# Attention and squared-ReLU MLP in one kernel: the last x rows copied on chip, plain x operands not stored, second weight group later, products in groups of 2, 3, 2

## The chip, the cores and the metric

One core of one Trainium2 chip. The metric is the device time of one execution in microseconds (us), as the median of several runs. TensorE (PE) multiplies, VectorE (DVE) and ScalarE (ACT) work elementwise, GpSimd (POOL) does elementwise work too, and SyncE (SP) issues the DMA transfers.

## The reference

```python
def _attn_ref(q, k, v, w1, b1, w2):        # q, k, v: 4 x 8 x 576 x 64
    scores = scale * np.matmul(q, k.transpose(0, 1, 3, 2))
    ...
    scores = scores + bias.transpose(2, 0, 1)[None, :, :, :]
    scores = scores - np.max(scores, axis=-1, keepdims=True)
    attn = np.exp(scores)
    attn = attn / (np.sum(attn, axis=-1, keepdims=True) + 1e-09)
    return np.matmul(attn, v)

def _moe_ref(x, w_in, w_out, s, b):        # x: 2304 x 512, w_in: 512 x 2048, w_out: 2048 x 512
    h = x @ w_in
    r = np.maximum(h, 0.0)
    g = s * (r * r) + b
    return g @ w_out
```

The attention's result, heads side by side, is the x of the second part.

## The kernel before

**Attention.** Heads and batches are worked off in 16 pairs of two batches of one head; `step(n)` issues a fifth of a pair for each of the engines. The last four pairs are (batches 0 and 1: head 6, head 7) and (batches 2 and 3: head 6, head 7). `norm_store` and `norm_load` (L327, L335) send the reciprocal row sums through memory (`rs`) and spread them over the partitions (`rb`). `av` (L409) multiplies by v in five groups of matmuls into `xps` (L422, L425); after the last group DVE multiplies by `rb` (L428, L429), and `store_xt` (L403) stores the result, transposed, as rows of `xt_d`.

**Second part.** The 2304 tokens are three pairs of chunks p = 0, 1, 2 of 768 tokens, the 2048 hidden units four groups g of 512. `items` lists the 12 steps (g, p): (0,0), (0,1), (1,1), (1,0) and so on. An item has two halves s, and a half is seven products in the order 1, 6, 5, 7, 2, 3, 4 (`ORDER`): a Strassen scheme in which x and w_in stand as seven operands each, four of them sums (T1 to T4 of x, S1 to S4 of w_in), three of them plain blocks (products 1, 2 and 3). Each operand is split into a high and a low part (ACT copies the high part, `x_hi` L587, `w_hi` L532; DVE subtracts, `x_lo` L591, `w_lo` L536), and a product (`product`, L604) is six matmuls of 384 columns at L614. `quad_posts` (L619) combines the four banks of a half: `keep` copies bank a before product 2 adds to it (ACT, L636), `u2` (DVE, L640), `v` reads bank b before product 3 adds to it (DVE, L645), `c22` reads bank d before product 4 adds to it (DVE, L648), and relu, square, affine and the split into `gt` follow. `project` (L711) multiplies `gt` by w_out: a block is three matmuls of 512 columns (L720), twelve blocks in each half of the following item. `evict` (L731) takes a finished `o` out of PSUM: ACT copies it in a chunk pair's first item (L738), DVE adds afterwards (L740).

**Operands and weights.** `load_x` (L559) loads a pair's x from `xt_d` into `x_in(p)`: into the weights' raw buffer `big` for p = 0, into `wd` otherwise. All seven split operands of p = 0 and 1 are stored to `xs_d` (`store_x`, 768 KB each) and come back by `reload_x` where a later item needs them. A weight group is loaded raw (`load_w`, L467), decoded in four passes (`decode_w`: ACT L476, POOL L478, DVE L480, L483, L486), and split; w_out's low part is POOL's (`wout_lo`, L507). Two buffers take turns for the decoded w_out, so the decoding of its third block waits for the low part of the first.

**The order.** It is written out by hand. The loop at L1087 counts slots T, seven to a half; a slot issues its product, its share of the twelve blocks (`SHARE`, L1086), and what `at(slot, ...)` has booked for it (`fire`). Item n starts at slot 14 n. A booking sets an instruction's place in its engine's queue; each engine works its queue in order and waits at an instruction whose inputs are not there. The first products of item 0 are issued between the last steps of the attention (L955 to L982).

Of the kernel before, what the change touches and what calls it, by code (L numbers as in the profile page):

```python
# [26 lines left out]
def attention_moe(ctx, tc, q, k, v, w_in, w_out, dist, par, out):  # L27
# [375 lines left out]
    def store_xt(p):  # L403
        h, b0 = pairs[p]
        xs = xts.pop(p)
        for x in range(2):
            nc.sync.dma_start(out=xt_d[b0 // 2][x, h * D:(h + 1) * D, :], in_=xs[64 * x:64 * x + 64, :])

# [150 lines left out]
    def load_x(p, a):  # L559
        t0, done = 2 * CH * p, 0  # L560
        while done < 2 * CH:
            b, o = divmod(t0 + done, S)
            w = min(2 * CH - done, S - o)
            nc.sync.dma_start(
                out=x_in(p)[:, a, done:done + w],
                in_=xt_d[b // 2][b % 2, 128 * a:128 * a + 128, o:o + w])
            done += w
# [387 lines left out]
    next(att)  # L955
    next(att)
# [32 lines left out]
    mix["wd"] = op.tile([128, 3, 1024], U32, name="wd")  # L989
# [12 lines left out]
    for n in range(1, NI + 1):  # L1002
        for j in range(2):
            for t, o in enumerate((4, 5, 7)):
                at(14 * n + 7 * j + o, lambda n=n, j=j, t=t: evict(n - 1, 1 - j, t), 0)

    def fresh_x(n, q, free):
        base = 14 * n
        for a in range(KB):
            at(base, lambda a=a: load_x(q, a))  # L1010
        for o, name in ((5, "T1"), (6, "T2"), (8, "T3"), (11, "T4")):
            for e in range(2):
                at(base + o, lambda name=name, e=e: x_sum(q, name, e, nc.vector, free))
        for i, m in enumerate(ORDER):
            o = base + (7 + i if i > 0 else 6)
            at(o, lambda m=m: x_new(q, m))
            for e in range(2):
                at(o, lambda m=m, e=e: x_hi(q, m, e))
            for e in range(2):
                at(o + 1, lambda m=m, e=e: x_lo(q, m, e, free))  # L1020
            if q < 2:
                at(o + 2, lambda m=m: store_x(q, m))

    def fresh_w(g):
        base = 28 * (g - 1)
        start = [base + (9 if g == 1 else 7), base + 20]
# [5 lines left out]
        for kind in range(2):  # L1032
            for i in range(4):
                k, t0 = 4 * kind + i, start[kind] + 3 * i
# [5 lines left out]
                if g == 1 and kind == 0:  # L1040
                    at(base + 4 + i // 2, lambda e=(kind, g, i): load_w(*e))
                elif g == 1 and i == 0:
                    at(base + 17, swap_raw, 1)
                    for x in range(3):
                        at(base + 17, lambda e=(kind, g, x): load_w(*e))
                elif g == 1 and i < 3:
                    pass
                else:
                    at(t0 - 7 if k < 3 else t0 - 6, lambda e=(kind, g, i): load_w(*e))
                at(t0 - 2, begin)  # L1050
                at(t0 - 1, lambda k=k: next(decs[k]))
                for x in range(3):
                    at(t0 + x, lambda k=k: next(decs[k]))
                if kind == 1:
                    at(t0 + 3, lambda i=i: wout_hi(g, i, nc.scalar))
                    at(t0 + 3, lambda i=i: wout_lo(g, i))
                    if g < 3:
                        at(t0 + 5, lambda i=i: store_wo(g, i))
        for name, o in (("S1", 21), ("S2", 21), ("S3", 24), ("S4", 26)):
            at(base + o, lambda name=name: w_sum(name, nc.vector), 1)  # L1060
        for i, m in enumerate(ORDER):
            at(base + 22 + i, lambda m=m: w_hi(m, nc.scalar))
            at(base + 23 + i, lambda m=m: w_lo(m, nc.vector))
            if g < 3:
                at(base + 25 + i, lambda m=m: store_wi(g, m))

    for i, m in enumerate(ORDER):
        at(i + 2, lambda m=m: store_x(0, m), 1)
# [3 lines left out]
    for n in range(1, NI - 1):  # L1072
# [4 lines left out]
        elif p1 != p:  # L1077
            for i, m in enumerate(ORDER):
                at(base + (7 + i if i > 0 else 2), lambda p1=p1, m=m: reload_x(p1, m))
# [6 lines left out]
    SHARE = (2, 2, 2, 2, 2, 1, 1)  # L1086
# [73 lines left out]
```

## Time and profile before

| | us |
|---|---|
| median of 3 runs | 671.68 (671.26 to 672.03) |
| the profiled execution | 668.71 |
| its span, first to last instruction | 666.8 |
| PE busy with matmuls | 635.6 (95%) |
| DVE busy | 500.7 (75%) |
| ACT busy | 437.5 (66%) |
| POOL busy | 184.0 (28%) |
| mean granted clock of PE | 0.985 |

The profile's page gives each engine's busy time, the span in 40 slices of 16.7 us, the chain of work that ended last, and the costliest groups of instructions by line. The timeline lists instructions in order of time; in brackets stands how long the engine was idle before one, and what ended that. An engine's next row starts where the one before it leaves the pipeline, so what an instruction costs in a busy stretch is the distance of two starts.

### The profile page before, as it was taken

To read this page: it belongs to the slowest core of one execution; us is meant where nothing else is said; L and a number is where in the kernel's file an instruction comes from. 1 tells how busy PE (TensorE), PEld (TensorE's weight loads), DVE (VectorE), ACT (ScalarE), POOL (GpSimd) and SP (SyncE) were. 2 spreads that over 40 slices of the span, in tenths; PEclk is the share of its full clock that TensorE was granted. 3 is DMA by queue.
4 is the path that set the end of the run, shared out by engine and by line. 5 is a ranking of instruction groups with operands and counts; after the bars stand their busy time and mean duration, and the time that the engine had idled before them with its cause. 6 is when DMAs were issued, how large, how long until landed. Compare 5 with 4: busy or idle time off the path is not lost.

```text
span 666.8 us, 14496 instructions
## 1 busy us (share of the span) xinstructions
PE 635.6 (95%) x5418; PEld 510.9 (77%) x5418; DVE 500.7 (75%) x1063; ACT 437.5 (66%) x927; POOL 184.0 (28%) x208
## 2 busy tenths in 40 slices
PE   8999989999999999759899999999999999999997
PEld 5667566666666665548788988889888898988886
DVE  7988888999999987666996798779648654445552
ACT  7988777888887787464886666457447544554440
POOL 7992332535668624011240122112100000000000
PEclk9999998999999999959999999999999999999999
DMA  6978688576877874699389269811361156546302
GB/s 183 329 236 280 211 268 279 170 259 208 278 262 248 268 246 149 202 402 389 142 321 385 85 251 328 314 57 61 140 240 48 64 197 229 180 167 204 144 0 95
DMA packets 54034, 142.00 MB, mean 213 GB/s; under 512 B 10445, under 2 KB 13517, under 8 KB 53965
## 3 DMA queue, kind: packets, MB, share of 16 engines
q1 hardware_dynamic: 53628, 140.82, 60.8%
q8 instruction: 43, 0.70, 0.4%
q10 hardware_dynamic: 208, 0.26, 0.1%
q14 instruction: 27, 0.21, 0.1%
q0 software_dynamic: 128, 0.00, 0.0%
HBM read 92.04 MB, written 49.02 MB: 212 GB/s over the span
## 4 chain that ended last, share of the span: by engine, by line
PE 70%; DMA 10%; DVE 8%; ACT 5%; issue 3%; POOL 3%; SPq 1%; DVEq 0%; ACTq 0%; POOLq 0%
PE o L720 28%; PE hps L614 23%; PE bps L170 5%; PE xps L422 5%; PE sps L277 5%; DMA qt<-in_q_dram 4%; PE tps L350 3%; ACT pr L310 3%; DMA big<-in_moe_w_in_dram 2%; DVE tt L299 1%; DMA wd<-in_moe_w_out_dram 1%; ACT pt L378 1%; DMA rs<-rt 1%; POOL kr L250 1%; DMA kt<-in_k_dram 1%
## 5 line engine op out<-in xcount | busy, mean ns | idle before, releaser
L720 PE MATMUL o<-wo,gt 128*128 128x512 f32 x864 | 224.9, 394 | 0.0
L614 PE MATMUL hps<-x,wi 128*128 128x384 f32 x1008 | 207.3, 342 | 14.0 <-ACT h L636 5.7
L614 PEld LDWEIGHTS hps<-x,wi 128*128 128x128 f32 x1008 | 182.7, 191 | 33.4 <-ACT h L636 6.2
L720 PEld LDWEIGHTS o<-wo,gt 128*128 128x128 f32 x864 | 159.7, 188 | 24.0 <-DVE gt L695 0.3
L310 ACT ACTIVATE pr<-tt,mn 128x576 f32<-128x576 f32 x144 | 110.7, 770 | 38.8 <-DVE mn L299 38.5
L299 DVE CUSTOM_DVE_ANT_0 tt<-sps,bt 128x576 f32<-128x576 f32 x128 | 91.4, 750 | 10.0 <-PE sps L277 8.7
L350 PEld LDWEIGHTS tps<-ident,pr 64*128 64x128 f32 x1216 | 44.5, 138 | 45.0 <-issue 20.1
L422 PE MATMUL xps<-pt,vt 128*64 128x256 f32 (+1 forms) x512 | 76.8, 421 | 1.0 <-PE xps L422 1.0
L277 PE MATMUL sps<-kr,qr 64*128 64x288 f32 x768 | 73.3, 309 | 3.1 <-POOL kr L250 2.7
L659 ACT ACTIVATE h<-hps 128x384 f32<-128x384 f32 x24 | 11.7, 488 | 83.8 <-PE hps L614 83.8
L277 PEld LDWEIGHTS sps<-kr,qr 64*128 64x128 f32 x768 | 58.9, 188 | 4.6 <-POOL kr L250 3.4
L350 PE MATMUL tps<-ident,pr 64*128 64x64 f32 x1216 | 56.1, 230 | 5.8 <-ACT pt L378 4.1
L678 ACT ACTIVATE h<-h,sb 128x384 f32<-128x384 f32 x72 | 50.8, 706 | 10.7 <-DVE h L674 9.3
L380 DVE COPY pt<-tps 128x512 f32<-128x512 f32 x64 | 43.8, 684 | 9.2 <-PE tps L350 8.7
L740 DVE TENSOR_TENSOR acc<-o,acc 128x512 f32<-128x512 f32 x36 | 24.8, 689 | 31.0 <-PE o L720 29.9
L422 PEld LDWEIGHTS xps<-pt,vt 128*64 128x64 f32 x512 | 31.2, 136 | 21.2 <-issue 9.5
L695 DVE TENSOR_TENSOR gt<-h,gt 128x384 fp32r<-128x384 f32 x72 | 41.6, 578 | 6.6 <-ACT gt L686 6.6
L170 PE MATMUL bps<-f,pt__127 128*32 128x79 f32 (+44 forms) x640 | 39.7, 390 | 2.2 <-POOL f L139 1.4
L686 ACT ACTIVATE gt<-h 128x384 fp32r<-128x384 f32 x72 | 37.8, 525 | 2.3
L137 DVE TENSOR_SCALAR f<-lg,thr 128x432 f32<-128x432 f32 (+9 forms) x68 | 39.2, 653 | 0.0
L170 PEld LDWEIGHTS bps<-f,pt__127 128*32 128x32 f32 x640 | 24.0, 109 | 17.9 <-issue 6.4
L378 ACT ACTIVATE pt<-tps 128x512 f32<-128x512 f32 x64 | 36.9, 577 | 0.0
(137 smaller groups left out, 798.8 us busy)
## 6 DMA issues: line engine op xcount, KB each, us to landing
x<-xs SPq DMA_DIRECT2D x21, 768.0 KB
wid<-wi SPq DMA_DIRECT2D x21, 512.0 KB
xs<-x SPq DMA_DIRECT2D x14, 768.0 KB
wi<-wid SPq DMA_DIRECT2D x21, 512.0 KB
bias<-stg SPq DMA_DIRECT2D x36, 295.5 KB
bt<-bias SPq DMA_DIRECT2D x7, 1152.0 KB
kt<-in_k_dram SPq DMA_DIRECT2D x16, 464.0 KB
wod<-wo SPq DMA_DIRECT2D x12, 512.0 KB
```

The costliest lines, as they stand in the source:

```text
L170: nc.tensor.matmul(pb[32 * c:32 * c + 32, base + a:base + b], w2bd, mov, start=True, stop=True)
L277: nc.tensor.matmul(o, a, b, start=(i == 0), stop=(i == 2))
L299: nc.vector.tensor_tensor_reduce(tt.rearrange("p (a b) -> p a b", a=2), ps[x][:, :, 0:HALF], bias.rearrange("p (a b) -> p a b", a=2), -1.0 ...
L310: nc.scalar.activation(pr[:, x], tts.pop((n, x)), AF.Exp, bias=mn[:, x:x + 1], scale=-1.0, accum_out=sums[p][:, col // 3, col % 3:col % 3 ...
L350: nc.tensor.matmul(outs[r], src[d], ident[d, d], is_transpose=True, start=start, stop=True, skip_group_check=not start)
L378: nc.scalar.activation(o, i, AF.Copy)
L380: nc.vector.tensor_copy(o, i)
L422: nc.tensor.matmul(o, vt[:, 4 * x + kb, :], pt[:, kb, x, c], start=(i == 0), stop=(i == 4))
L614: nc.tensor.matmul(ps, w_ops[m][:, w, k, s], xo[p, m][:, x, k], start=(first and i == 0), stop=(i == 5), skip_group_check=not first)
L678: return lambda: nc.scalar.activation(tmp[fo, j], tmp[fo, j], AF.Identity, bias=b_, scale=s_)
L695: nc.vector.tensor_tensor(lo, tmp[fo, j], hi, op=ALU.subtract)
L720: nc.tensor.matmul(os_t[t], gt[:, a, tok], w[:, b], start=(fo == 0 and i == 0), stop=(fo == 3 and i == 2))
```

## The change

- `store_xt` also books copies from SBUF to SBUF (`direct_x`, `copy_x`): the rows of heads 6 and 7 in chunk pair 0, and those of batch 2 in chunk pair 1, go into `x_in` without memory between.
- The other x rows of chunk pair 1 are loaded during the attention's last steps: `wd` is allotted earlier for that, and the eighth x buffer later.
- The three plain operands are not stored. `reload_x` loads their x rows from `xt_d`, and `split_hi` (ACT) and `split_lo` (DVE), each on 768 columns, split them again.
- The last steps of the attention come ahead of the first products: two products, not four, stand ahead of the last `av` group's end.
- The bookings of weight group 1 move: w_in's loads from slots 4 and 5 to slot 7, its decoding from slots 9 to 20 to slots 15 to 23, w_out's decoding from 20 to 31 to 25 to 32, the sums and splits of w_in by three slots; a few bookings of x sums by one or two.
- `SHARE` puts the twelve blocks behind the second, fifth and seventh product, four at each place.

```diff
@@ store_xt
             nc.sync.dma_start(out=xt_d[b0 // 2][x, h * D:(h + 1) * D, :], in_=xs[64 * x:64 * x + 64, :])
+        if h >= H - 2:
+            direct_x(h, b0, xs)
+
+    def direct_x(h, b0, xs):
+        r = slice(64 * (h % 2), 64 * (h % 2) + 64)
+        if b0 > 0:
+            late_x.append((x_in(1)[r, KB - 1, CH:2 * CH], xs[0:64, 0:CH]))
+        else:
+            late_x.append((x_in(0)[r, KB - 1, 0:S], xs[0:64, :]))
+            late_x.append((x_in(0)[r, KB - 1, S:2 * CH], xs[64:128, 0:2 * CH - S]))
+    def copy_x():
+        while late_x:
+            o, i = late_x.pop(0)
+            nc.sync.dma_start(out=o, in_=i)
@@ reload_x
-        nc.sync.dma_start(out=xo[p, m].bitcast(F32), in_=xs_d[p][m - 1])
+        if isinstance(X_OPS[m], str):
+            nc.sync.dma_start(out=xo[p, m].bitcast(F32), in_=xs_d[p][m - 1])
+            return
+        k, j = X_OPS[m]
+        t0 = 2 * CH * p + CH * (j - 1)
+        for e in range(2):
+            load_tokens(xo[p, m][:, 1, e].bitcast(F32), 2 * k - 2 + e, t0, t0 + CH)
+    def split_hi(p, m):
+        t = xo[p, m]
+        nc.scalar.activation(t[:, 0], t[:, 1].bitcast(F32), AF.Copy)
+    def split_lo(p, m):
+        t = xo[p, m]
+        nc.vector.tensor_tensor(t[:, 1], t[:, 1].bitcast(F32), t[:, 0].bitcast(F32), op=ALU.subtract)
@@ the attention's last steps
-        if n == LAST - 4:
-            load_x(0, KB - 1)
+        if n == LAST - 5:
+            copy_x()
-    free_x.extend(xp.tile([128, 2, 2, CH], F32R, name=f"x{i}") for i in range(8))
+    free_x.extend(xp.tile([128, 2, 2, CH], F32R, name=f"x{i}") for i in range(7))
+    mix["wd"] = xp.tile([128, 3, 1024], U32, name="wd")
     next(att)
+    for a in range(KB):
+        load_x(1, a, 0, 2 * CH if a < KB - 1 else CH)
     next(att)
...
+    for _ in range(3):
+        next(att)
+        copy_x()
+    next(att)
     prep(1)
     prep(6)
-    next(att)
     product(0, 0, 1, False)
     prep(5)
+    product(0, 0, 6, False)
     next(att)
-    product(0, 0, 6, False)
+    store_xt(NP - 1)
+    copy_x()
     fire(1)
     prep(7)
-    next(att)
     product(0, 0, 5, False)
     fire(2)
     prep(2)
-    prep(3)
-    next(att)
     product(0, 0, 7, False)
     fire(3)
+    prep(3)
     prep(4)
-    next(att)
-    store_xt(NP - 1)
@@ fresh_w, the bookings of weight group 1
-        start = [base + (9 if g == 1 else 7), base + 20]
+        first = g == 1
+        passes = [base + 7 + k for k in range(12)] + [base + 20 + k for k in range(12)]
+        if first:
+            passes[0:12] = [15 + (3 * k) // 4 for k in range(12)]
+            passes[12:24] = [25 + (2 * k) // 3 for k in range(12)]
...
-                    at(base + 4 + i // 2, lambda e=(kind, g, i): load_w(*e))
+                    at(7, lambda e=(kind, g, i): load_w(*e))
...
+        d = 3 if first else 0
...
-            at(base + 22 + i, lambda m=m: w_hi(m, nc.scalar))
-            at(base + 23 + i, lambda m=m: w_lo(m, nc.vector))
+            at(base + 22 + d + i, lambda m=m: w_hi(m, nc.scalar))
+            at(base + 23 + d + i, lambda m=m: w_lo(m, nc.vector))
@@ the loop
-    SHARE = (2, 2, 2, 2, 2, 1, 1)
+    SHARE = (0, 4, 0, 0, 4, 0, 4)
```

What this moves on SP at the attention's end. Ahead of the last pair's row sums (`rs15`) stood one load of the last x rows of chunk pair 0; `big` and `wd` are the places of the x rows of chunk pairs 0 and 1, `rb` are finished x rows or, loaded from `rs`, the spread row sums. Before, from the row sums on:

```order
L331 DMA rs15_115<-rt_5246 4x128
L333 DMA rs15_115<-rt_5246 1x64
L331 DMA rs15_115<-rt_5246 4x128
L333 DMA rs15_115<-rt_5246 1x64
L338 DMA rb_5285<-rs15_115 64x576 x2
L407 DMA xt1_122<-rb_5092 64x576 x2
L407 DMA xt1_122<-rb_5285 64x576 x2
L564 DMA wd_5383<-xt0_121 128x384
L564 DMA wd_5383<-xt1_122 128x384
L564 DMA wd_5383<-xt0_121 128x384
```

Now, from the last load of chunk pair 1 on (six more such loads and two copies stand right ahead):

```order
L585 DMA wd_5200<-xt0_121 128x384
L331 DMA rs15_115<-rt_5255 4x128
L333 DMA rs15_115<-rt_5255 1x64
L331 DMA rs15_115<-rt_5255 4x128
L333 DMA rs15_115<-rt_5255 1x64
L338 DMA rb_5286<-rs15_115 64x576 x2
L407 DMA xt1_122<-rb_5094 64x576 x2
L424 DMA wd_5200<-rb_5094 64x384
L407 DMA xt1_122<-rb_5286 64x576 x2
L424 DMA wd_5200<-rb_5286 64x384
L617 DMA xs0_116<-x1_5194 128x1536
```

The loads into `wd` went from behind the last pair's row sums to in front of them, and one copy is what is left behind.

On ACT in the second half of item 0, around `keep` (`h0<-hps`). Before, the first decoding pass of group 1's w_in (`wf<-big`) stood in front of it:

```order
L587 ACTIVATE x7_5198<-wd_5383 128x384 x2
L678 ACTIVATE h2_5267<-h2_5267,sb_124 128x384
L686 ACTIVATE gt2_5376<-h2_5267 128x384
L666 ACTIVATE h1_5266<-h1_5266 128x384
L476 ACTIVATE wf_1021<-big_134 128x512
L636 ACTIVATE h0_5265<-hps_5447 128x384
L669 ACTIVATE h1_5266<-h1_5266 128x384
```

Now:

```order
L608 ACTIVATE x7_5394<-wd_5200 128x384 x2
L713 ACTIVATE h2_5276<-h2_5276,sb_124 128x384
L721 ACTIVATE gt2_5387<-h2_5276 128x384
L701 ACTIVATE h1_5275<-h1_5275 128x384
L671 ACTIVATE h0_5274<-hps_5440 128x384
L704 ACTIVATE h1_5275<-h1_5275 128x384
```

The decoding pass left this place; it now comes twenty instructions further back.

On ACT around the switch to weight group 1 (`wi1`, `wi6`, ... are the operands of products 1, 6, ..., `wo1` those of w_out, `f` its decoding, `acc` evicted results). Before, from `keep` of the second half of item 1 on:

```order
L636 ACTIVATE h0_5265<-hps_5693 128x384
L669 ACTIVATE h2_5267<-h2_5267 128x384
L678 ACTIVATE h2_5267<-h2_5267,sb_124 128x384
L686 ACTIVATE gt6_5380<-h2_5267 128x384
L495 ACTIVATE wi1_1010<-wf_1021 128x512
L495 ACTIVATE wo10_5367<-f0_5394 128x512
L495 ACTIVATE wi6_1011<-big_134 128x512
L476 ACTIVATE f0_5394<-wd_5383 128x512
L495 ACTIVATE wi5_1012<-s2_5384 128x512
L738 ACTIVATE acc0_5385<-o_5700 128x512
L495 ACTIVATE wi7_1013<-big_134 128x512
```

Now, from `keep` of the first half of item 2 on, one half later:

```order
L671 ACTIVATE h2_5276<-hps_5819 128x384
L704 ACTIVATE h1_5275<-h1_5275 128x384
L713 ACTIVATE h1_5275<-h1_5275,sb_124 128x384
L721 ACTIVATE gt5_5390<-h1_5275 128x384
L512 ACTIVATE wo11_5379<-f1_5406 128x512
L493 ACTIVATE f1_5406<-wd_5200 128x512
L512 ACTIVATE wi2_1014<-wf_1021 128x512
L512 ACTIVATE wi3_1015<-s2_5395 128x512
```

The operand of product 2 is now made inside the half that uses it, and right ahead of it stands a pass (`f1<-wd`) into the buffer that POOL's low part of `wo11` frees.

## Rows read from the trace of the kernel before

**Rows 1.** The page, part 2: PE's granted clock in 40 slices of the span
```profile
PEclk9999998999999999959999999999999999999999
```

**Rows 2.** Windows: stretch, length, busy us (instructions) of PE, PEld, DVE, ACT, POOL, clock, DMA
```profile
100.00:103.50 3.50, 3.50 (x32) 2.37 (x30) 2.11 (x8) 2.54 (x8) 0.00 (x0) 0.52 0.92 315
...
281.00:298.00 17.00, 8.17 (x23) 6.94 (x24) 10.87 (x23) 9.22 (x21) 1.81 (x2) 0.50 1.01 402
...
326.00:330.00 4.00, 2.43 (x12) 1.89 (x11) 4.00 (x7) 2.79 (x6) 1.88 (x2) 1.00 0.84 315
```

**Rows 3.** Timeline of PE, the attention's end and item 0: start, us, instruction [idle before]
```profile
262.05 1.32 PE L614 MATMUL hps<-x,wi 128*128 128x384 f32 x6
263.29 1.19 PE L422 MATMUL xps<-pt,vt 128*64 128x256 f32 x8
...
269.99 1.19 PE L422 MATMUL xps<-pt,vt 128*64 128x256 f32 x8
271.11 5.47 PE L614 MATMUL hps<-x,wi 128*128 128x384 f32 x30
279.34 1.34 PE L614 MATMUL hps<-x,wi 128*128 128x384 f32 x6 [2.75 <-DVE h L652]
282.37 2.29 PE L614 MATMUL hps<-x,wi 128*128 128x384 f32 x6 [1.69 <-DVE h L655]
290.37 2.29 PE L614 MATMUL hps<-x,wi 128*128 128x384 f32 x6 [5.71 <-ACT h L636]
```

**Rows 4.** Timeline of PE, item 1 and the first product of item 2
```profile
303.23 1.21 PE L614 MATMUL hps<-x,wi 128*128 128x384 f32 x6
304.27 1.55 PE L720 MATMUL o<-wo,gt 128*128 128x512 f32 x6
305.66 1.20 PE L614 MATMUL hps<-x,wi 128*128 128x384 f32 x6
...
314.15 1.22 PE L614 MATMUL hps<-x,wi 128*128 128x384 f32 x6
315.22 1.55 PE L720 MATMUL o<-wo,gt 128*128 128x512 f32 x6
...
328.67 1.32 PE L614 MATMUL hps<-x,wi 128*128 128x384 f32 x6 [1.57 <-DVE h L645]
...
332.81 1.22 PE L614 MATMUL hps<-x,wi 128*128 128x384 f32 x6
```

**Rows 5.** Timeline of ACT, items 0 and 1
```profile
272.91 0.52 ACT L666 ACTIVATE h<-h 128x384 f32<-128x384 f32 x1
...
275.19 0.60 ACT L684 ACTIVATE gt<-h,sb 128x384 fp32r<-128x384 f32 x1
...
289.27 0.66 ACT L476 ACTIVATE wf<-big 128x512 f32<-128x512 f32 x1 [6.40 <-DMA big<-in_moe_w_in_dram]
...
327.30 0.67 ACT L476 ACTIVATE f<-wd 128x512 f32<-128x512 f32 x1 [0.93 <-POOL wo L507]
```

**Rows 6.** Timeline of DVE, the attention's end and item 0
```profile
271.23 0.42 DVE L428 TENSOR_TENSOR rb<-xps,rb 128x256 f32<-128x256 f32 x1 [0.29 <-PE xps L422]
...
281.29 0.56 DVE L578 TENSOR_TENSOR acc<-wd,acc 128x384 f32<-128x384 f32 x1 [0.68 <-DMA wd<-xt]
...
282.23 0.55 DVE L695 TENSOR_TENSOR gt<-h,gt 128x384 fp32r<-128x384 f32 x1
```

**Rows 7.** Timeline of SP, the attention's end: transfers issued
```profile
260.62 0.25 SPq L333 DMA_DIRECT2D rs<-rt  x1
262.71 1.11 SPq L338 DMA_DIRECT2D rb<-rs  x2
...
273.26 3.87 SPq L564 DMA_DIRECT2D wd<-xt  x8
```

**Rows 8.** Timeline of POOL, item 1 and item 2: w_out's low parts
```profile
325.93 1.33 POOL L507 TENSOR_TENSOR wo<-f,wo 128x512 fp32r<-128x512 f32 x1 [2.36 <-ACT wo L495]
...
332.61 2.71 POOL L507 TENSOR_TENSOR wo<-f,wo 128x512 fp32r<-128x512 f32 x1 [3.94 <-ACT wo L495]
```

More of the change, by code (lines that the diff above doesn't have):

```diff
@@ L557, in x_in, with load_x, load_tokens @@
         return mix["wd"].bitcast(F32).rearrange("p a b -> p (a b)").rearrange("p (a b) -> p a b", a=4)
[L559 to L563, printed above, removed]
+    def load_x(p, a, lo=0, hi=768):
+        t0 = 2 * CH * p
+        load_tokens(x_in(p)[:, a, lo:hi], a, t0 + lo, t0 + hi)
+    def load_tokens(o, a, t0, t1):
+        done = t0
+        while done < t1:
+            b, off = divmod(done, S)
+            w = min(t1 - done, S - off)
             nc.sync.dma_start(
-                out=x_in(p)[:, a, done:done + w],
-                in_=xt_d[b // 2][b % 2, 128 * a:128 * a + 128, o:o + w])
+                out=o[:, done - t0:done - t0 + w],
+                in_=xt_d[b // 2][b % 2, 128 * a:128 * a + 128, off:off + w])
             done += w
@@ L1003, in attention_moe @@
         for j in range(2):
-            for t, o in enumerate((4, 5, 7)):
+            for t, o in enumerate((5, 7, 7)):
                 at(14 * n + 7 * j + o, lambda n=n, j=j, t=t: evict(n - 1, 1 - j, t), 0)
@@ L1008, in fresh_x @@
         base = 14 * n
-        for a in range(KB):
+        for a in range(KB) if q > 1 else ():
             at(base, lambda a=a: load_x(q, a))
-        for o, name in ((5, "T1"), (6, "T2"), (8, "T3"), (11, "T4")):
+        for o, name in ((7, "T1"), (8, "T2"), (10, "T3"), (12, "T4")):
             for e in range(2):
@@ L1020, in fresh_x @@
                 at(o + 1, lambda m=m, e=e: x_lo(q, m, e, free))
-            if q < 2:
+            if q < 2 and isinstance(X_OPS[m], str):
                 at(o + 2, lambda m=m: store_x(q, m))
@@ L1033, in fresh_w @@
             for i in range(4):
-                k, t0 = 4 * kind + i, start[kind] + 3 * i
+                k, (t0, t1, t2) = 4 * kind + i, passes[12 * kind + 3 * i:12 * kind + 3 * i + 3]
                 def begin(k=k, e=(kind, g, i)):
@@ L1038, in begin @@
                     next(decs[k])
-                if g == 1 and kind == 0:
-                    at(base + 4 + i // 2, lambda e=(kind, g, i): load_w(*e))
-                elif g == 1 and i == 0:
-                    at(base + 17, swap_raw, 1)
+                if first and kind == 0:
+                    at(7, lambda e=(kind, g, i): load_w(*e))
+                elif first and i == 0:
+                    at(17, swap_raw, 1)
                     for x in range(3):
[L1045 to L1049, printed above, removed]
+                        at(17 + x, lambda e=(kind, g, x): load_w(*e))
+                elif not (first and i < 3):
+                    at(t0 - 4 if first else t0 - 7 if k < 3 else t0 - 6, lambda e=(kind, g, i): load_w(*e))
@@ L1050, in fresh_w @@
                 at(t0 - 2, begin)
                 at(t0 - 1, lambda k=k: next(decs[k]))
-                for x in range(3):
-                    at(t0 + x, lambda k=k: next(decs[k]))
+                for t in (t0, t1, t2):
+                    at(t, lambda k=k: next(decs[k]))
                 if kind == 1:
-                    at(t0 + 3, lambda i=i: wout_hi(g, i, nc.scalar))
-                    at(t0 + 3, lambda i=i: wout_lo(g, i))
+                    at(t2 + 1, lambda i=i: wout_hi(g, i, nc.scalar))
+                    at(t2 + 1, lambda i=i: wout_lo(g, i))
@@ L1064, in fresh_w @@
             if g < 3:
-                at(base + 25 + i, lambda m=m: store_wi(g, m))
+                at(base + 25 + d + i, lambda m=m: store_wi(g, m))
     for i, m in enumerate(ORDER):
-        at(i + 2, lambda m=m: store_x(0, m), 1)
+        if isinstance(X_OPS[m], str):
+            at(4 + i // 2, lambda m=m: store_x(0, m), 1)
     fresh_x(0, 1, x_free[0])
@@ L1078, in attention_moe @@
             for i, m in enumerate(ORDER):
-                at(base + (7 + i if i > 0 else 2), lambda p1=p1, m=m: reload_x(p1, m))
+                o = base + (7 + i if i > 0 else 2)
+                at(o, lambda p1=p1, m=m: reload_x(p1, m))
+                if not isinstance(X_OPS[m], str):
+                    at(o + 3, lambda p1=p1, m=m: split_hi(p1, m))
+                    at(o + 4, lambda p1=p1, m=m: split_lo(p1, m))
         if g1 < g:
```

8 lines of the change are left out of this document (5 added, 3 removed).

## The prediction

> **What bounds the kernel now.** I read the clock by slices first: PE is at full clock nearly everywhere, and one slice two fifths into the span stands at 5 [rows 1]. The windows give that place its size: from 281 to 298 us the granted clock was 0.50, 1.2 GHz, and PE was busy for 8.17 of 17 us [rows 2]. The timeline of PE says what came before it: after five products in a row PE waited 2.75 us, then 1.69, then 5.71 us [rows 3]. The last of these is a wait for ACT's `keep`, and ACT stood in front of it, at the first decoding pass of weight group 1, for 6.40 us, because that pass's w_in had not landed [rows 5]. The waits of 2.75 and 1.69 us are for `c12` and `c21` on DVE, which stood behind sums of x rows that were still on their way: the second of four such sums waited until 281.29 for loads issued from 273.26 on [rows 6, 7].
>
> Behind item 0, PE is a dense row. A product there costs 304.27 - 303.23 = 1.04 us, two blocks 305.66 - 304.27 = 1.39, and a product behind a single block 315.22 - 314.15 = 1.07 [rows 4]. At 1.04 for each of seven products and 1.39 for each of six double blocks a half takes 7.28 + 8.34 = 15.62 us. From the second half of item 1 (its first product starts at 314.15) to item 2 (332.81) it took 18.66, so 3.0 us are lost there, 1.57 of them in a wait for DVE's `v` [rows 4].
>
> So there are two places to win at, item 0 and the end of item 1. What lies behind them is PE's own time.
>
> **The end of the attention.** In the kernel before, the last group of `av` starts at 269.99, and DVE multiplies by the row sums 1.24 us later, at 271.23 [rows 3, 6]. Four products of 1.24 us each (263.29 - 262.05, [rows 3]) lie between the groups. Now two lie there, one of them right behind the other at 1.04: 4 x 1.24 - 2.28 = 2.7 us sooner, so 268.55. But seven loads into `wd` now stand on SP ahead of the row sums, at 3.87 / 8 = 0.48 us each [rows 7]. Before, the last sum went out at 260.62 and its way back began at 262.71; I put both some 1.8 us later, and take 269.0 for the multiplication.
>
> **From there to item 1.** DVE now has 36 operations from this multiplication to `c22` of the second half, in front of the half's last product, since the low parts of four x operands have come to stand behind it. At 0.47 us each (two steps from 281.29 to 282.23, [rows 6]) they take 16.9 us, and 1.1 us of waiting for ACT's chain of relu, square and copy come in (four steps in 2.28 us, 272.91 to 275.19, [rows 5]): `c22` ends at 287.0. PE waits in front of the second half's products 2, 3 and 4, by some 0.9, 2.7 and 1.3 us. One product later, at 288.1, item 1 begins, and its second half at 288.1 + 15.62 = 303.7, where it was 314.15: **10.4 us sooner**. The decoding pass is gone from in front of `keep`. Its data now stands on SP behind four stores of x operands, from 271 on: these eight transfers, 5.2 MB at the 402 GB/s of [rows 2], take 13 us, and ACT asks for the first of them near 292. The transfers that fall away (six stores of x operands, half of nine reloads) are hidden behind PE on either side, so I count them as nothing; their cover is a half's 15.6 us, and the seven transfers of a reload, 5.5 MB, take 13.7 at that rate. The copies from SBUF to SBUF save a store and a load for the last rows, but the sum that reads them now comes at 280 us behind DVE's own row, so they too are worth nothing by themselves. The new splits are nine of about 0.9 us each on ACT and on DVE, two or three in a half of 15.6 us, three slots behind their loads and four ahead of their products: hidden; if that cover were gone, 0.9 us each.
>
> **Item 1 to item 2.** The first half of item 1 needs the decoded x only, and by DVE's and ACT's order nothing is late. The 3.0 us lost before at the end of item 1 go, since less decoding lies ahead of `v`. What is late next is weight group 1 itself. Its splits moved by three slots. In the second half of item 1 (start H) ACT waits for a finished `o` behind the second four blocks, until H + 10.9 (five products, eight blocks and 0.1). From there to the high part of product 2's operand it has 24 instructions in its queue at about 0.54 us (0.57 in the chain above), 13.0 us, and two waits of at least 1.33 us each for POOL's low part of w_out, which now come right ahead of decoding passes (one such wait was 0.93 us before, [rows 5, 8]). That is H + 26.7; DVE's low part takes 0.7 more. Product 2 of item 2 would be due at H + 15.62 + 6.94 (four products, four blocks) = H + 22.5. So PE waits **4.9 us** there, in two or three pieces, of which the longest is about 3.4. POOL's operation took 2.71 us beside a busy DVE [rows 8], so the bounds are 4.9 and 4.9 + 2 x 1.38 = 7.7; I take 5.3, near the lower one, because DVE itself stands idle in the second of the two waits.
>
> **The clock.** Waits of 2.75 and 1.69 us with a product between them were followed by the fall at 281; a single wait of 1.57 us left the clock at 1.00 [rows 2, 3]. The new waits in item 0 (2.7 and 1.3) and in item 2 (3.4) resemble the former, so I count a fall for each. In this trace the clock also fell for a short stretch, 100.0 to 103.5, with PE busy throughout: at half speed that costs 1.75 us [rows 2]. The bounds for one fall are 0 and half of 17 us. I take 1.0 in item 0, where part of the low stretch is waiting anyway, and 1.7 in item 2. By the Trainium skill ("TensorE: Matmul & The Clock Gate", section "HAM oscillation — how this bites in real kernels") what takes the clock down is one long idle gap, and none of the new gaps would be long enough; by that rule the sum below would be better by these 2.7 us. The trace disagrees for item 0: no wait before 281 was longer than 2.75 us, and the clock fell.
>
> **The groups of products.** PE's price of a product or a block is the same in any group, except that two products in each half no longer stand behind a single block: 2 x (1.07 - 1.04) = 0.06 us, in 21 halves 1.3 at most, 0 at least. I take 0.9. Later evictions cost nothing: the four blocks behind a half's fifth and seventh product hide them.
>
> **The sum.** -10.4 (item 0) - 3.0 (end of item 1) + 5.3 (weights late) + 2.7 (clock) - 0.9 (groups) = **-6.3 us**. Against the profiled execution of 668.7 us this is 662.4. The median of the runs shown is 671.7, 3.0 us above the profiled one; the change is the same, so I forecast **665.4 us**.
>
> **The rivals.**
>
> *The weights are in time* (0.22). ACT's queue may run faster than I count, and w_in's splits may slip in under PE's blocks. Then 5.3 and 1.7 fall away: -6.3 - 7.0 = -13.3, 658.4 us. For it: ACT is busy for 66% only, and before, the splits were ready half an item ahead. Against it: the wait at H + 10.9 is there whatever ACT's speed, and the two waits for POOL stand right behind it.
>
> *The clock does not fall* (0.10). If a product between the waits is enough to hold it, as the skill's rule has it, -9.0: 662.7 us. The row that speaks against it is named above.
>
> *The row sums are late* (0.13). The loads into `wd` of before were waited for until 281.29, 4.2 us behind the last of their issues at 277.1 [rows 6, 7], twice the 2.1 of the row sums' first leg. If each of the row sums' two legs takes that, the multiplication comes at 273.2, everything behind it 4.2 us later: -2.1, 669.6 us.
>
> *Slower* (0.09): the clock stays low through item 2. The wait for product 2 is there in any case; if PE then goes on in short pieces, each waiting for a split, the clock may stay at half for as long as it did at 281, 17 us, and PE, busy for most of it, loses up to 8.5 us instead of 1.7. With the upper bound for POOL (+2.4) that is -6.3 + 6.8 + 2.4 = +2.9, 674.6 us. It decides from about 13 us at half clock on. Against it: the splits of products 3 and 4 come right behind that of product 2, so PE is dense again after one product.
>
> That the change does not do what it says is excluded by the order of the queues, except for the groups, whose gain is near nothing in any case.
>
> **How the numbers follow.** My forecast, with a range of its own of 662 to 668.5, has 0.46. A measurement of this kernel tells 0.2% (1.3 us) from no change. Faster than that are the forecast, the first two rivals and most of the third: 0.84. Within it lie the rest of the third and the lower part of the fourth: 0.08. Slower: 0.08. The range reaches from the first rival to the third with a margin for the bounds, 657.5 to 671; below it lies less than a tenth, above it a little more than one.
>
> **What would show it.** The first product of item 1 starts near 288; the fall of the clock near 281 gives way to a shorter one; ACT's wait for w_in of 6.40 us is gone, and with it PE's 5.71. In front of product 2 of item 2 PE waits some 3.4 us for DVE's low part, behind ACT, behind POOL. A half behind item 2 takes 15.62 to 15.65 us. I am wrong if item 1 starts after 293, or if PE runs through the switch to group 1 without a wait.

## The result, and the profile after

Four runs of the changed kernel took 660.78 to 664.46 us, median 663.34; four of the kernel before 671.26 to 673.48, median 671.86. The ratio is 0.986, 95% interval 0.983 to 0.990. Forecast were 665.4 us in a range of 657.5 to 671.0: the direction and the range held, the gain is 8.5 us where 6.3 were forecast.

The profiled execution took 664.46 us with a span of 662.6, only 4.2 us less than the profiled one of before. The two traces differ ahead of the change's place too, so distances are taken from one instruction, called S: the start of the first of the last five `av` groups (the texts put on record before the runs call it the start of the last attention group). It is a row of `xps` behind an idle time of 0.97 us, at 260.93 us in the profile of before and 265.04 after. From S to the end of the span it was 405.92 us, and is 397.55: 8.4 us less.

The clock by slices, and windows of the trace after (columns as in [rows 2]):

```profile
PEclk9999999999999799989989999999999999999999
```
```profile
282.00:292.00 10.00, 7.09 (x30) 5.95 (x29) 9.88 (x22) 8.98 (x21) 0.00 (x0) 0.83 1.01 374
322.00:345.00 23.00, 19.34 (x84) 15.91 (x83) 19.38 (x30) 15.12 (x29) 7.71 (x7) 0.93 0.85 313
345.00:640.00 295.00, 295.00 (x1475) 266.32 (x1474) 200.48 (x357) 171.10 (x319) 26.98 (x24) 1.00 0.47 164
```

The slice at 5 of [rows 1] is gone. In the two stretches around item 0's end and around the switch to weight group 1 PE is idle for 2.91 and 3.66 us, and the clock fell for a part of each: the records of the trace show it at 0.50 for 3.41 us from 288.28 on and for 3.41 from 336.07, where the trace of before has 17.07 us from 281.07 on. From 345 us to its last matmul PE has no idle time at all.

Two rows of PE before, S and the last wait of item 0, and then its timeline after, at the places of [rows 3, 4]:

```profile
260.93 1.19 PE L422 MATMUL xps<-pt,vt 128*64 128x256 f32 x8 [0.97 <-PE xps L422]
...
294.41 5.16 PE L614 MATMUL hps<-x,wi 128*128 128x384 f32 x18 [1.75 <-DVE h L645]
```

```profile
265.04 2.16 PE L439 MATMUL xps<-pt,vt 128*64 128x256 f32 x16 [0.97 <-PE xps L439]
...
272.36 5.40 PE L649 MATMUL hps<-x,wi 128*128 128x384 f32 x24
278.59 5.45 PE L649 MATMUL hps<-x,wi 128*128 128x384 f32 x30 [0.83 <-DVE h L683]
284.19 1.31 PE L649 MATMUL hps<-x,wi 128*128 128x384 f32 x6 [0.16 <-ACT h L671]
287.90 1.98 PE L649 MATMUL hps<-x,wi 128*128 128x384 f32 x6 [2.39 <-DVE h L680]
290.24 4.05 PE L649 MATMUL hps<-x,wi 128*128 128x384 f32 x18 [0.36 <-DVE h L683]
...
323.30 1.58 PE L649 MATMUL hps<-x,wi 128*128 128x384 f32 x8
325.86 0.97 PE L649 MATMUL hps<-x,wi 128*128 128x384 f32 x4 [0.98 <-DVE wi L553]
...
331.27 0.96 PE L649 MATMUL hps<-x,wi 128*128 128x384 f32 x4 [0.26 <-DVE wi L553]
334.54 1.74 PE L649 MATMUL hps<-x,wi 128*128 128x384 f32 x6 [2.31 <-ACT wi L512]
```

The waits of 2.75, 1.69 and 5.71 us of [rows 3] and the one of 1.75, 11.9 us in all, have become 0.83, 0.16, 2.39 and 0.36, 3.7 in all; new are three in item 2, for weight operands (`wi`). Item 1 starts at 292.04 (the seventh matmul of the row at 290.24), S + 27.0 where it was S + 37.4 (the thirteenth of the row at 294.41); its second half at 307.66, item 2 at 323.30. Of these 10.4 us, 8.2 are idle time of PE; in the other 2.3 the same matmuls take less time, with the clock at 0.50 for 3.41 us in place of 17.07.

The same stretch on DVE and on SP:

```profile
272.47 0.42 DVE L445 TENSOR_TENSOR rb<-xps,rb 128x256 f32<-128x256 f32 x1 [4.72 <-DMA wd<-rb]
...
281.93 1.02 DVE L599 TENSOR_TENSOR acc<-wd 128x384 f32<-128x384 f32 x2
```
```profile
260.87 3.19 SPq L585 DMA_DIRECT2D wd<-xt  x7
264.17 0.27 SPq L331 DMA_DIRECT2D rs<-rt  x1
...
267.89 1.11 SPq L338 DMA_DIRECT2D rb<-rs  x2
...
278.54 4.85 SPq L484 DMA_DIRECT2D big<-in_moe_w_in_dram  x4
```

The multiplication by the row sums stands at S + 7.43, before at S + 10.30 [rows 6]. And ACT at the switch, where [rows 5] had one wait of 0.93 us:

```profile
318.63 0.60 ACT L773 ACTIVATE acc<-o 128x512 f32<-128x512 f32 x1 [4.87 <-PE o L755]
...
324.69 0.69 ACT L493 ACTIVATE f<-wd 128x512 f32<-128x512 f32 x1 [1.40 <-POOL wo L524]
...
333.30 0.67 ACT L493 ACTIVATE f<-wd 128x512 f32<-128x512 f32 x1 [1.75 <-POOL wo L524]
333.88 0.61 ACT L512 ACTIVATE wi<-wf 128x512 fp32r<-128x512 f32 x1
```

It is the chain that the prediction laid out: a wait for the finished `o` 11.0 us behind the start of the half (307.66), two waits for POOL's low part of w_out, and behind the second one the high part of product 2's operand.

### The profile page after: what moved, and what is told of

Same layout as the page of the kernel before. It is cut to its first block, busy times and chain, and to the rows that moved or that the text cites. A ratio compares the mean times of both kernels' runs of the same rounds, so it can differ in the third digit from the quotient of the medians.

```text
span 662.6 us, 14551 instructions
## 1 busy us (share of the span) xinstructions
PE 635.9 (96%) x5418; PEld 511.9 (77%) x5418; DVE 507.9 (77%) x1072; ACT 443.9 (67%) x936; POOL 184.6 (28%) x208
## 4 chain that ended last, share of the span: by engine, by line
PE 73%; ACT 7%; DVE 7%; DMA 6%; issue 3%; POOL 2%; SPq 1%; DVEq 0%; ACTq 0%; POOLq 0%
PE o L755 29%; PE hps L649 24%; PE bps L170 5%; PE sps L277 5%; PE xps L439 5%; PE tps L350 4%; ACT pr L310 3%; DVE tt L299 2%; DMA rs<-rt 2%; DMA qt<-in_q_dram 2%; ACT pt L378 1%; DVE pt L380 1%; DMA big<-in_moe_w_in_dram 1%; DMA kt<-in_k_dram 1%; DVE x L612 1%
## 5 line engine op out<-in xcount | busy, mean ns | idle before, releaser
L755 PE MATMUL o<-wo,gt 128*128 128x512 f32 x864 | 210.9, 394 | 0.0
L649 PE MATMUL hps<-x,wi 128*128 128x384 f32 x1008 | 191.8, 339 | 7.5 <-DVE h L680 2.4
L649 PEld LDWEIGHTS hps<-x,wi 128*128 128x128 f32 x1008 | 178.8, 189 | 17.3 <-DVE h L680 2.7
L755 PEld LDWEIGHTS o<-wo,gt 128*128 128x128 f32 x864 | 162.4, 189 | 31.7
```

The source lines that it names most:

```text
L649: nc.tensor.matmul(ps, w_ops[m][:, w, k, s], xo[p, m][:, x, k], start=(first and i == 0), stop=(i == 5), skip_group_check=not first)
L755: nc.tensor.matmul(os_t[t], gt[:, a, tok], w[:, b], start=(fo == 0 and i == 0), stop=(fo == 3 and i == 2))
```

## The experiments

There are twelve runs. Ten take the changed kernel and undo or add one to three things; the other two are the changed kernel and the kernel before, once more. This table sets their profiles side by side (us). "Mult." is the multiplication by the last row sums, "item 1" the start of its first product, both from S on; then come the two halves of item 1, the first half of item 2, and the distance from S to the end of the span. All are starts of single instructions in the traces.

| profile | S | mult. | item 1 | its halves | item 2, first half | end |
|---|---|---|---|---|---|---|
| before | 260.93 | 10.30 | 37.42 | 15.81, 18.66 | 15.69 | 405.92 |
| before again | 263.19 | 10.52 | 37.99 | 15.98, 18.34 | 15.69 | 406.33 |
| changed | 265.04 | 7.43 | 27.00 | 15.62, 15.64 | 21.99 | 397.55 |
| changed again | 265.64 | 7.45 | 27.30 | 16.15, 15.64 | 20.41 | 396.79 |
| weights back | 258.42 | 9.86 | 31.20 | 16.70, 16.01 | 15.64 | 396.87 |
| x loads back | 264.30 | 7.43 | 27.28 | 16.10, 15.64 | 20.41 | 396.77 |
| groups back | 261.10 | 10.76 | 30.60 | 17.57, 15.69 | 19.07 | 401.13 |
| x ahead | 263.21 | 8.82 | 24.93 | 15.61, 15.64 | 21.96 | 395.43 |
| weights sooner | 262.67 | 7.53 | 27.09 | 15.74, 15.64 | 16.52 | 392.28 |
| x ahead, weights sooner | 262.65 | 10.32 | 26.81 | 16.00, 15.64 | 16.53 | 392.26 |
| all stored | 263.38 | 7.44 | 26.80 | 15.62, 15.64 | 21.96 | 397.76 |
| both, sums first | 265.31 | 7.46 | 25.06 | 17.30, 15.64 | 16.51 | 391.82 |
| weights and x loads back | 264.46 | 7.45 | 31.95 | 17.37, 15.64 | 15.64 | 398.00 |
| the same, slots back | 261.17 | 7.43 | 30.09 | 16.14, 16.65 | 15.64 | 395.87 |

**The changed kernel again.** 

> The changed kernel again, as the standard for the runs beside it. Expected: 662 to 664 us, that is 8 to 10 us under the kernel before. All halves of item 3 and later 15.64 us; item 0 from the start of the last attention group's first product of P x V to item 1's first product 27.0 us; item 2's first half 21.99 us. Theory: the 4.1 us by which the profiled attention ended later than before belong to that one execution (a late load of queries at 207 to 214 us and a clock at 0.5 for 6.8 us behind it); then the last group starts near 261 here. Rival: they belong to the change; then it starts near 265 again.

Median 662.96 us of six (660.83 to 667.32), ratio 0.989 (0.985 to 0.993). Its distances agree with the first profile's to within 0.8 us, but S is late again, at 265.64: the rival holds so far. Item 2's first half has the same three waits of 0.98, 0.26 and 2.31 us, without a fall of the clock at the switch: 20.41 us. So the fall cost 1.58 us, the waits with what they leave behind them 20.41 - 15.64 = 4.77.

**Weights back.** `fresh_w(1)` as before: w_in loaded at slots 4 and 5, first pass at slot 9, splits at slot 22.

```diff
-            passes[0:12] = [15 + (3 * k) // 4 for k in range(12)]
-            passes[12:24] = [25 + (2 * k) // 3 for k in range(12)]
...
-        d = 3 if first else 0
+        d = 0
```

> Of the changed kernel, only the booking of weight group 1 is put back to that of the kernel before (loads, decoding passes, splits). My theory: the late weights cost 6.35 us in front of item 2 and save less than that elsewhere. Item 2's first half falls from 21.99 to 15.64 us; the first decoding pass stands again in front of keep in item 0 and two passes (1.8 us of DVE each) in front of the half's last product, so item 1 begins 2 to 4 us later, and its second half loses 0 to 3 us. In all -3 to 0 us against the changed kernel. Rival 1: the late weights save nothing in item 0: -6 us. Rival 2: they are what the gain of item 0 hangs on: item 1 begins 6 us later or more and loses 3 us at its end, in all +2 us or more.

Median 660.71, ratio 0.985 (0.981 to 0.988). The stall in front of item 2 is gone (15.64), item 1 begins 4.2 us later and takes 32.71 us in place of 31.26. Of the 4.2, the late multiplication (S + 9.86) accounts for 2.4: see the groups below. From S to the end it is 396.87, as the changed kernel's. My theory holds, at its upper end: the late weights save about what they cost. The second half of item 1 takes 16.01 us with the old booking too, where the kernel before needs 18.66.

**The x loads back**, to slot 0, the last rows by way of DRAM again.

```diff
...
-    for a in range(KB):
-        load_x(1, a, 0, 2 * CH if a < KB - 1 else CH)
...
-        for a in range(KB) if q > 1 else ():
+        for a in range(KB):
```

> Of the changed kernel, only the loads of the second pair's x are put back to slot 0, behind the stores of the last attention rows, and its last rows go by way of DRAM again. My theory: the first sum of these rows is asked for at 282 us of the changed kernel's trace and its data, issued from 275 on, is there by then or a little after: 0 to +1.5 us. Rival: the early loads are what removed PE's waits of 2.75 and 1.69 us: +4 us or more, and DVE waits for the DMA in front of the second sum as before.

Median 663.41, ratio 0.988 (0.985 to 0.991). DVE's sums and PE's wait in this kernel's timelines:

```profile
281.19 1.02 DVE L597 TENSOR_TENSOR acc<-wd 128x384 f32<-128x384 f32 x2
...
283.53 1.02 DVE L597 TENSOR_TENSOR acc<-wd,acc 128x384 f32<-128x384 f32 x2
```
```profile
287.16 1.32 PE L647 MATMUL hps<-x,wi 128*128 128x384 f32 x6 [2.38 <-DVE h L678]
```

No sum waits for data, PE's waits are those of the changed kernel, item 1 starts at S + 27.28. My theory holds and the rival falls: loading the second pair's x sooner is worth nothing here, beside the late weights.

**Groups back.** `SHARE = (2, 2, 2, 2, 2, 1, 1)`, evictions at slots 4, 5, 7.

> Of the changed kernel, only the grouping of products and blocks is put back (2, 2, 2, 2, 2, 1, 1 blocks behind the seven products, evictions at slots 4, 5, 7). My theory: a half takes 15.69 us in place of 15.64, in 18 undisturbed halves +0.85, with the end +1.0 us. Rival 1: the groups are worth nothing (the halves stay at 15.64): 0. Rival 2: the first eviction of a half is asked for two slots sooner, so ACT comes sooner to the weights' high parts and the 6.35 us in front of item 2 shrink by 1 to 2 us: in all 0 to -1 us.

Median 662.29, ratio 0.988 (0.985 to 0.991). Both the theory and its second rival came true: every later half takes 15.69 us, 0.047 more, and the switch costs 19.07 - 15.69 = 3.38 us in place of 4.77. The two cancel. The profile shows something else as well, in SP's and DVE's timelines:

```profile
260.32 4.51 SPq L585 DMA_DIRECT2D wd<-xt  x7
264.94 0.27 SPq L331 DMA_DIRECT2D rs<-rt  x1
...
268.10 1.11 SPq L338 DMA_DIRECT2D rb<-rs  x2
```
```profile
271.85 0.42 DVE L445 TENSOR_TENSOR rb<-xps,rb 128x256 f32<-128x256 f32 x1 [5.48 <-DMA xt<-rb]
```

The seven loads held SP until S + 3.7, the row sums went out at S + 3.8, and the multiplication stands at S + 10.76. Nothing in this kernel's order up to here differs from the changed one, but the loads began at S - 0.8, where they began at S - 4.2 in the changed kernel. Of the eight profiles with these loads ahead of the row sums, four have the sums late (8.82 to 10.76), four on time (7.43 to 7.53). The four late ones are those whose loads began at S - 2.5 or later; in the four on time they began at S - 3.7 or sooner. In the four without them ahead, it is 7.43 to 7.46 each time.

**x ahead.** The last four operands are split in front of the multiplication.

```diff
     product(0, 0, 6, False)
+    prep(7)
+    prep(2)
+    prep(3)
+    prep(4)
     next(att)
```

> Of the changed kernel, only this: the last four x operands of pair 0 are split ahead of the multiplication by the row sums, into DVE's wait of 4.72 us there, and not behind it. My theory: DVE's queue between the multiplication and c22 of item 0's second half is what PE waits for (0.83, 0.16, 2.39 and 0.36 us); it gets 8 operations of 0.47 us shorter, so these 3.7 us go but for some tenths, and with them the fall of the clock at 288 us (1.7 us): -3 to -5 us. Rival: the sums of the second pair's x are bound by the DMA of its last rows, which starts only behind the multiplication; then the queue waits there instead and it is -1 us or nothing.

Median 659.50, ratio 0.984 (0.981 to 0.988). The waits of 0.83 and 0.16 us are gone, that of 2.39 stays, the fall of the clock too (284.24). Item 1 at S + 24.93, 2.1 us sooner although the sums were 1.4 us late. From S to the end it is 2.1 us less than in the first profile of the changed kernel, which has the same two falls of the clock behind S: between the rival and the theory. The medians differ by 3.5. The wait of 2.39 is not this queue's length alone.

**Weights sooner.** Two loads of weight group 2 also go out three slots later.

```diff
-            passes[0:12] = [15 + (3 * k) // 4 for k in range(12)]
-            passes[12:24] = [25 + (2 * k) // 3 for k in range(12)]
+            passes[0:12] = [15 + (2 * k) // 3 for k in range(12)]
+            passes[12:24] = [25 + (2 * k) // 3 + 2 * (k > 5) for k in range(12)]
...
-                    at(t0 - 4 if first else t0 - 7 if k < 3 else t0 - 6, lambda e=(kind, g, i): load_w(*e))
+                    at(t0 - 4 if first or g == 2 and k in (1, 2) else t0 - 7 if k < 3 else t0 - 6, lambda e=(kind, g, i): load_w(*e))
...
-        d = 3 if first else 0
+        d = 2 if first else 0
```

> Of the changed kernel, only the slots of weight group 1 are changed: w_in's passes end one slot sooner (slot 22), sums and splits of w_in come one slot sooner, and w_out's third and fourth operand are decoded two slots later, behind w_in's splits, so that ACT does not wait for POOL's low parts in front of them. My theory: the 6.35 us in front of item 2 are this queue of ACT's; they fall to 0 to 1.5 us, the clock does not fall at 336 us: -4.8 to -6.3 us. Rival: the splits are bound by ACT's wait for the eviction at 10.9 us of the half or by DVE, which is full in item 1's first half: the stall keeps 3 us or more, or item 1 gets slower by as much.

Median 658.86, ratio 0.984 (0.980 to 0.988). ACT and PE at the switch:

```profile
327.72 0.66 ACT L493 ACTIVATE f<-wd 128x512 f32<-128x512 f32 x1
...
328.80 0.62 ACT L512 ACTIVATE wi<-wf 128x512 fp32r<-128x512 f32 x1
330.89 0.68 ACT L493 ACTIVATE f<-wd 128x512 f32<-128x512 f32 x1 [1.47 <-DMA wd<-in_moe_w_out_dram]
```
```profile
331.91 1.22 PE L649 MATMUL hps<-x,wi 128*128 128x384 f32 x6
333.77 1.28 PE L649 MATMUL hps<-x,wi 128*128 128x384 f32 x6 [0.64 <-DVE h L683]
```

The last high part of w_in's operands (`wi<-wf`, 328.80) now stands ahead of ACT's wait of 1.47 us for w_out's data, none of PE's waits is for `wi`, and item 2's first half takes 16.52 us: 5.5 less than in the profile of the changed kernel, 3.9 less than in its second one. Item 1 got no slower (15.74, 15.64). The theory holds: the stall at the switch is that queue of ACT's, but for the 0.9 us that stay (16.52 - 15.64), with a wait of 0.64 for DVE.

**Both.** 

> The edits of the two runs before this one together. My theory: the two places do not touch each other, so the gains add up: -8 to -11 us against the changed kernel, 652 to 656 us. Rival: with item 1 starting sooner, w_in's raw data is not there when the first pass is asked for, and ACT waits in front of keep: less than the sum by 2 us or more.

Median 654.02 of six (651.88 to 658.12), ratio 0.977 (0.973 to 0.980): 2.3% under the kernel before, and its interval lies wholly below those of the changed kernel. In the profile the gain of the operands put ahead doesn't show: the row sums were late (S + 10.32), and the end, 392.26 from S, is that of the run before. So from S on the profiles show 5 of the 9 us between the medians. The profiled execution itself took 656.69 us, 2.7 above its median, and its S is 2.4 to 3.0 us sooner than in the two profiles of the changed kernel; the rest stays open.

**All stored.** The plain operands stored and reloaded split, without the new splits.

> Of the changed kernel, only this is undone: the plain x operands of pairs 0 and 1 are stored and reloaded split, as before, in place of being loaded plain and split again. My theory: six stores and the other halves of nine reloads are hidden behind PE: 0 us, within 0.5, every half 15.64. Rival: the stores hold up the loads of w_in and w_out behind them on the same queue (three more of 0.8 to 1.3 us ahead of w_out's): the first decoding pass of w_out waits, and item 2's first half gets longer by 1 us or more.

Median 664.58, ratio 0.992 (0.989 to 0.995). 397.76 us from S, with the same fall of the clock at the switch, against 397.55. As expected: nothing, in this booking of the weights.

**Both, and the row sums first on SP.** The loop with the seven loads stands behind the third `next(att)`, in which the way back of the sums is issued.

> The run with both edits (x operands ahead, weights sooner), and in addition the seven loads of the second pair's x go behind the way back of the last row sums on SP's queue, where they stood ahead of the sums' way out. My theory: in the traces so far the sums go out between 1.7 us before and 3.8 us behind the start of the last attention group, with the loads ahead of them 3.2 to 5.5 us on the queue; the multiplication follows 7.43 us behind that start where PE decides, up to 10.75 where the sums are late. Now it is 7.4 in every execution, and the loads still land before the first sum asks for them: 1 to 3 us less than the run with both edits at the median, 651 to 653 us, and a smaller spread. Rival: the loads come too late and DVE waits for them in front of the first sums; then nothing is gained.

Median 657.26, ratio 0.979 (0.974 to 0.984): not better than the run with both edits, and I had expected 651 to 653. The mechanism came: multiplication at S + 7.46, item 1 at S + 25.06. But the clock stayed low for 6.83 us from 287.3 on and item 1's first half took 17.30 us; 391.82 from S. Which of the two is better, these runs don't tell.

**The kernel before again.** 

> The kernel before, once more with a profile. The question is the attention: its last group started at 260.9 us in the first profile of this kernel, and between 258.4 and 265.6 in nine profiles of the changed kernel and its variants, all with the same order of instructions up to 250 us. Theory: that spread is one of executions (a load of queries that lands late at 200 to 220 us) and this profile falls into it, at 258 to 266. Rival: the change itself puts these waits there by way of its memory layout; then this one is at 261 again, and without waits of PE over 1 us between 195 and 225 us.

Ratio 1.001 (0.998 to 1.004). PE's waits from 195 to 225 us (us in total, times, the longest), first of this kernel, then of the changed one:

```profile
PE sps L277 <- POOL kr L250: 1.1, 2, 0.6
PE tps L350 <- DVE pt L380: 0.6, 1, 0.6
```
```profile
PE sps L277 <- POOL kr L249: 2.5, 1, 2.5
PE sps L277 <- POOL kr L250: 1.8, 2, 1.2
PE tps L350 <- DVE pt L380: 0.5, 1, 0.5
```

S is 263.19, inside the spread of 258.42 to 265.64. But neither profile of before has a wait over 0.6 us there, while ten of twelve with the change have one over 1 us, and each of those ten has a fall of the clock between 203 and 223 us. Behind it stands POOL, waiting for queries (`qt`) up to 6.9 us in the profile of the changed kernel, up to 5.4 in those of before. SP issues the same transfers in the same order up to there. Neither theory is shown.

**Weights and x loads back.** The second and the third experiment's edits together.

> Of the changed kernel, both the booking of weight group 1 and the loads of the second pair's x are put back. Alone, the first cost item 0 some 2 us besides late row sums, the second nothing; the changed kernel's item 1 begins 27.0 us behind the start of the last attention group, that of the kernel before 37.4. Theory A: the 10.4 us hang on both together, since x's loads now stand ahead of w_in's on SP and ACT stands at the first decoding pass in front of keep: item 1 at 33 to 36 us. Theory B: each acts by itself and the rest of the 10.4 us comes from the order of the attention's end and the later slots of x's sums: item 1 at 29 to 31 us.

Median 662.60, ratio 0.988 (0.984 to 0.992). Item 1 at S + 31.95, between the two theories, 1 us from either. Its second half takes 15.64 us, with the old booking of the weights. PE waits for `keep`, behind ACT's first pass, as in [rows 3], but shorter:

```profile
287.34 2.29 PE L647 MATMUL hps<-x,wi 128*128 128x384 f32 x6 [3.85 <-ACT h L669]
```

**The same, with the sums' slots back.** 5, 6, 8, 11 in place of 7, 8, 10, 12.

> The run before this one (weights and x loads put back), and the sums of the second pair's x go back to slots 5, 6, 8 and 11. Theory: the sums then stand on DVE ahead of c12 and c21 of item 0's first half and wait there for their data, so PE waits in front of the second half's first products by 2 to 4 us more: item 1 begins 3 to 5 us later than in the run before this one, 34 to 36 us behind the start of the last group. Rival: the slots are worth nothing, since DVE has the same work until c22 of the second half: within 1 us of the run before.

Median 659.77, ratio 0.985 (0.980 to 0.989). Both failed: item 1 comes 1.9 us sooner, not later. On SP and ACT:

```profile
274.61 0.38 SPq L615 DMA_DIRECT2D xs<-x  x1
275.08 1.75 SPq L482 DMA_DIRECT2D big<-in_moe_w_in_dram  x2
```
```profile
281.71 0.67 ACT L491 ACTIVATE wf<-big 128x512 f32<-128x512 f32 x1 [1.50 <-DMA big<-in_moe_w_in_dram]
```

w_in's loads go out at S + 13.9 (in the kernel before at S + 18.6, behind three stores of x operands, here one), and ACT's wait of 6.40 us [rows 5] is 1.50, with the old bookings of weights, x loads and sums. In the run before this one the loads go out at S + 13.9 too, and that wait is 3.05 us; why it is shorter here isn't shown. With all three put back the end is 395.87 from S, no later than the changed kernel's.

## Why the prediction was right, and where not

The sum, by the means of the two profiles of each kernel:

| term | forecast | measured |
|---|---|---|
| item 0, to the second half of item 1 | -10.4, clock +1.0 | 53.60 to 43.03: -10.6 |
| end of item 1 | -3.0 | 18.50 to 15.64: -2.9 |
| weights late | +5.3 | 20.41 - 15.64 = +4.8 |
| clock in item 2 | +1.7 | +1.6 in one profile, 0 in the other |
| groups | -0.9 | 18 x 0.047 and 0.2 at the end: -1.05 |
| sum | -6.3 | -9.0 |

**Item 0** came at the time forecast: DVE's queue from the multiplication to `c22` sets the start of item 1, 19.6 us behind the multiplication where 19.1 were forecast (16.1 in the run that takes eight operations out of that queue), and PE waits in front of products 2, 3 and 4 for 0.16, 2.39 and 0.36 us, where 0.9, 2.7 and 1.3 were expected. The term mis-sized here is the clock: its fall came, and the whole is -10.6 where -10.4 + 1.0 were forecast. That DVE's queue sets the time with the fall too, so that 1.0 was counted twice, is argued: no profile is without this fall. The multiplication came 0.6 us sooner (7.43 behind S; 269.0 was 8.07).

**The end of item 1** gave the 3.0 us forecast, but not for the reason given, that less decoding lies ahead of `v`: with the weights booked as before, the half takes 16.01, 15.64 and 16.65 us in three runs, not 18.5. What else in the edit removed the loss was not run apart.

**The second term mis-sized** is the clock in item 2: I charged 1.7 us in any case, and with the same waits of 0.98, 0.26 and 2.31 us it fell in three profiles of five (changed, x ahead, all stored) and not in two (changed again, x loads back). The price of a fall was right. For item 0 the fall came in all fourteen profiles, in those with the change with a longest wait of 1.8 to 3.9 us ahead of it. So "the clock does not fall" was no case for item 0. The rule that the prediction weighed (the Trainium skill, "TensorE: Matmul & The Clock Gate", section "HAM oscillation — how this bites in real kernels": one long idle gap) does not hold here: in eight profiles the fall came with no wait above 2.39 us.

**The weights** came late by the chain forecast, and the lower bound was the right end. That it hangs on ACT's queue behind POOL's low part is shown by the run that shortens it: 20.41 to 16.52. The pieces lay otherwise than forecast: 0.98 and 0.26 us inside products 6 and 7, and 2.31 in front of product 2, where 3.4 were expected.

**The rival of late row sums** was under-priced in its chance. I gave it 0.13; it came in four of the eight profiles with the loads ahead, at 1.4 to 3.3 us, not 4.2. The two of the changed kernel itself were on time. **Slower** (a low clock through item 2) came in none: the longest stretch there was 3.41 us. **Groups and stores** came as sized for the halves; what I missed is that the groups also move ACT's wait for `o`, worth 1.4 us against the change at the switch.

**What failed is part of the cause that I read into the sum.** I took the gain of item 0 to be the decoding pass taken away from in front of `keep`. The runs divide it otherwise. Weights late against early, with late x loads: 31.95 to 27.28, 4.7 us; given back by 4.8 to 6.35 in item 2. The x loads: 0 beside the late weights; beside the early ones item 1 comes 0.75 us sooner with them (31.20 against 31.95), although the row sums were late there. Later slots of the sums: 1.9 against the change, measured in the old booking. What remains, 37.4 or 38.0 to 30.1, 7.3 us or more, is in the rest of the edit: the new order of the attention's end, which brings the multiplication 2.9 us forward and the loads behind it with it, the copies for the first pair, and the plain operands that aren't stored ahead of w_in's loads. These three were not run apart (only the stores, with late weights, where they are worth nothing). The traces of the kernel before and of the last run show where the time lies: `keep` comes at S + 21.1 where it came at S + 28.9; w_in's loads go out 4.7 us sooner, 2.9 of it with the multiplication, and ACT's first pass starts 6.6 us behind them where it was 9.8. Which of the three does how much of that stays open. So x loaded sooner and weights later earn nothing together (398.00 us from S without both, 397.55 and 396.79 with them); the gain of item 0 is in the rest.

## What to carry to other kernels

Before believing a sum of terms, undo them one by one and in pairs: a part may be worth 4.7 us at one place and cost it at the next. A bulk load put ahead of a small transfer with a round trip (here row sums to DRAM and back) cost nothing where the load began early enough and up to 3.3 us where it didn't. Putting the small one first brought the sums on time, though this run showed no better median for it. And when an operand is made in the half that uses it, look at what its engine must wait for just ahead of it: moving two decoding passes behind the splits, and the splits a slot forward, took 3.9 to 5.5 us off the switch without any new work.

## What the runs showed of the hardware that I had not expected

The same seven loads on SP's queue took 3.19 to 5.45 us to issue, from profile to profile of the same order; what parts the late row sums from the others is rather when the loads began, 3.7 to 4.2 us ahead of S in those on time and 0.8 to 2.5 in the late ones. Where the row sums behind them went out 3.6 us or more after S (three profiles), the multiplication came 2.4 to 3.3 us late. The clock fell or held after the same waits of PE (0.98, 0.26 and 2.31 us at the switch: three profiles and two). And S varied by 7.2 us (258.42 to 265.64) among programs with one order of transfers up to there; whether the change makes late ones more likely stays open.
